# Block-sparse attention with a fused FFN: gathering only the needed K and V blocks, worked off in thirds of a batch

## The chip, the cores and the metric

The kernel runs on one core of a Trainium2 chip. The metric is the device time of one execution in microseconds (us), smaller is better. Each run also records the clock that was granted to the matmul engine (1.00 is full speed), and a run more than 1.5% above the fastest of its kernel counts as "slow".

The engines are named as in the profile: PE does matmuls (PEld is its weight load), DVE and ACT are the vector and the scalar engine, POOL is the engine that also issues gathers, SP issues most DMAs (its queue q1 moves 37.3 of 47.7 MB in the changed kernel). Each engine has its own list of instructions; in the traces below PE stands for 6.94 us before one of them while others stand behind it in the list.

## The reference

```python
# B, H, S, D = 4, 8, 768, 64;  block = 32, so 24 blocks;  3 sampled blocks for each query block
scores = q @ k.T / sqrt(D)
mask   = |blk_i - blk_j| <= 1  or  blk_i or blk_j is the first or last block
mask  |= (blk_j in sampled_blocks[blk_i])
attn   = softmax(where(mask, scores, -1e9)) @ v          # [4, 8, 768, 64]
x      = attn, heads side by side                        # [3072, 512]
h      = x @ w_in                                        # [3072, 1024]
solu   = h * softmax(h)
ln     = (solu - mean) / sqrt(var + 1e-6) * g_ln
out    = ln @ w_out                                      # [3072, 512]
```

q, k and v are drawn at a tenth of a normal distribution. The scores are therefore tiny and the softmax weights nearly equal over the allowed keys. A kernel that uses the wrong K or Q, or K of another batch, still passes the comparison.

## The kernel before

It computes all scores, masked ones too. The mask comes in through the matmul: K and Q are stored transposed with 24 extra rows (a block selector in K, minus 30000 for masked blocks in Q), so a masked score comes out of the same matmul as a large negative number. All is worked off in thirds of a batch (256 query rows), four pairs of heads in each, and the FFN of the third before is slipped in piece by piece.

```python
    def transpose_pair(b, pr):
        i = b % 2
        kc, qc, vc = loaded.pop((b, pr))
        for src, dst in ((kc, kT[i]), (qc, qT[i])):
            tp = ps_m.tile([P, S], BF16, tag="m", name="tp")
            for c in range(NCH):
                nc.tensor.matmul(tp[:, c * P : (c + 1) * P],
                                 src[:, c, :, :], ident,
                                 is_transpose=True, start=(c == 0),
                                 stop=(c == NCH - 1))
            nc.vector.tensor_copy(out=dst[0:D, 0, pr, :], in_=tp[0:D, :])
            nc.vector.tensor_copy(out=dst[D:P, 1, pr, :], in_=tp[D:P, :])
        nc.vector.tensor_copy(out=va[i][:, 2 * pr : 2 * pr + 2, :, 0:D],
                              in_=vc)

    # ... cut ...
    def scores(b, t, pr, n, exs):
        i = b % 2
        s = ps_s.tile([P, 4, TW], FP32, tag="s", name="s")
        for m in range(4):
            hh, jc = divmod(4 * n + m, NCH)
            nc.tensor.matmul(s[:, m, :],
                             kT[i][rows[hh], hh, pr, jc * P : (jc + 1) * P],
                             qT[i][rows[hh], hh, pr, t * TW : (t + 1) * TW],
                             start=(m % 2 == 0), stop=(m % 2 == 1))
        e = expp.tile([P, 4, TW], BF16, tag="ex", name="ex")
        nc.scalar.activation(out=e, in_=s, func=ACT.Exp, scale=scale)
        exs.append(e)

    # ... cut ...
    def pv(b, t, pr, exs, x):
        i = b % 2
        op = ps_m.tile([P, 2, 2, D + 1], FP32, tag="m", name="op")
        first = True
        for n in range(3):
            for m in range(4):
                hh, jc = divmod(4 * n + m, NCH)
                for qt in range(2):
                    nc.tensor.matmul(op[:, qt, hh, :],
                                     exs[n][:, m, qt * P : (qt + 1) * P],
                                     va[i][:, 2 * pr + hh, jc, :],
                                     start=first,
                                     stop=(n == 2 and m == 3 and qt == 1),
                                     skip_group_check=True)
                    first = False
    # ... cut ...
    # main loop, for each unit of a third and a pair of heads:
            if un in (2, 4, 6, 8):
                loaded[(b + 1, (un - 2) // 2)] = load_pair(b + 1, (un - 2) // 2)
            if un in (5, 7, 9, 11):
                bg.append(lambda b=b, p=(un - 5) // 2: transpose_pair(b + 1, p))
    # ... cut ...
        nbg = -(-len(bg) // 5) if len(bg) else 0
        for n in range(3):
            scores(b, t, pr, n, exs)
            if n == 0 and prev is not None:
                pb, pt, ppr, pexs = prev
                pv(pb, pt, ppr, pexs, xs[(pb, pt)])
                if ppr == NPR - 1:
                    bg.extend(ffn_pieces(pb, pt, xs[(pb, pt)]))
            if bg:
                bg.popleft()()
```

The preparation of the next batch is simple: Pool issues 20 loads for each batch that cast to bf16 on the way (`load_pair`), PE transposes K and Q, DVE copies them into place. No gather comes into it.

The softmax here doesn't subtract the row's maximum and nothing guards it: scores larger than these inputs give would overflow.

## Time and profile before

| | before |
|---|---|
| median of the first 3 runs (lowest to highest) | 281.83 us (281.5 to 283.57) |
| span of the profiled run | 281.1 us |
| PE busy | 238.8 us, 85% |
| PE not busy | 42.3 us, 28 of them in the first 60 us, 7 in the last 21 |
| one third of a batch in the middle | 19.5 us |

These lines are from the page of the kernel before. The first gives busy time by engine. The next four cut the span into 40 equal slices (7 us each); a digit is the busy share in tenths, and for PEclk the granted clock in tenths. Then come the DMA queue that Pool's issues go to (packets, MB, share of the time of 16 engines), and the chain of work that ended last, by engine.

```profile
PE 238.8 (85%) x3163; PEld 183.2 (65%) x3177; DVE 157.9 (56%) x365; ACT 174.4 (62%) x206; POOL 82.8 (29%) x142
PE   0116686999999999999999999999999999899783
ACT  1002468548858859667677688588488595785630
PEclk9999999999999999999999999999999999999998
DMA  5999999409759810049279020090100200200202
q0 software_dynamic: 55056, 10.49, 45.8%
PE 62%; DMA 11%; ACT 10%; DVE 9%; issue 3%; POOL 3%; ACTq 0%; POOLq 0%
```

The second view is the table by stretches of the same kernel. Columns: stretch and its length, then busy time (and instructions) of PE, PEld, DVE, ACT and POOL, the granted clock, the DMA share and GB/s.

```profile
core 0: us, PE busy (x) PEld busy (x) DVE busy (x) ACT busy (x) POOL busy (x), PEclk, DMA share, GB/s
60.00:100.00 40.00, 38.97 (x539) 30.13 (x541) 26.02 (x60) 28.52 (x34) 18.54 (x29) 1.00 0.85 87
100.00:140.00 40.00, 38.69 (x523) 29.81 (x525) 21.25 (x51) 28.58 (x34) 10.63 (x20) 1.00 0.42 53
140.00:180.00 40.00, 38.40 (x523) 29.67 (x523) 21.41 (x50) 28.64 (x34) 9.28 (x17) 1.00 0.39 48
180.00:220.00 40.00, 39.29 (x546) 30.60 (x546) 25.18 (x57) 28.79 (x34) 5.89 (x12) 1.00 0.24 38
```

And the waits of PE between 60 and 140 us, in the same kernel: who waited for whom, total us, times, longest.

```profile
PE s L215 <- ACT ex L220: 0.7, 3, 0.2
PE op L231 <- ACT ex L220: 0.4, 1, 0.4
```

Read together: from 60 us on PE has something to do in 38.4 to 39.3 of each 40 us, at full clock, and waits for nothing worth naming. PE is the limit there. ACT, at 28.6 of 40, and DVE, at 21 to 26, are not. Only work taken off PE can shorten the middle.

### The profile page before, as it was taken

Reading aid. Unit: us, or ns where it says so; the run is one execution under the profiler, and the core shown is the slowest. Engines: PE = TensorE matmul, PEld = TensorE weight load, DVE = VectorE, ACT = ScalarE, POOL = GpSimd, SP = SyncE. Lnnn points to the kernel's source line nnn. Section 1 sums busy time; section 2 is a strip of 40 time slices with the busy share of each in tenths; the row PEclk is TensorE's granted clock in tenths of the full one; section 3 lists DMA queues with packets and bytes.
Section 4 is the critical chain, followed back from the end, with each engine's and each line's share of the span. In section 5 each row is a group of like instructions: output and inputs, shape, how many; then the busy total and the mean of one; then the engine's idle time right before and its main releaser. Section 6 shows DMA issues by size and latency. Waiting matters only on the chain.

```text
span 281.1 us, 7445 instructions
## 1 busy us (share of the span) xinstructions
PE 238.8 (85%) x3163; PEld 183.2 (65%) x3177; DVE 157.9 (56%) x365; ACT 174.4 (62%) x206; POOL 82.8 (29%) x142
## 2 busy tenths in 40 slices
PE   0116686999999999999999999999999999899783
PEld 0004564867867867867767768678678577686561
DVE  3079789648639622756666616386376236155261
ACT  1002468548858859667677688588488595785630
POOL 8695861218139110045253100140100101001001
PEclk9999999999999999999999999999999999999998
DMA  5999999409759810049279020090100200200202
GB/s 117 264 191 188 185 180 118 58 4 140 48 93 128 85 54 23 2 90 100 30 109 79 3 77 2 37 96 2 47 31 2 77 2 2 76 2 3 76 0 77
DMA packets 61636, 20.40 MB, mean 73 GB/s; under 512 B 52225, under 2 KB 56994, under 8 KB 61602
## 3 DMA queue, kind: packets, MB, share of 16 engines
q0 software_dynamic: 55056, 10.49, 45.8%
q1 hardware_dynamic: 6546, 9.43, 9.8%
q8 instruction: 25, 0.41, 0.6%
q14 instruction: 9, 0.07, 0.1%
HBM read 23.07 MB, written 6.29 MB: 104 GB/s over the span
## 4 chain that ended last, share of the span: by engine, by line
PE 62%; DMA 11%; ACT 10%; DVE 9%; issue 3%; POOL 3%; ACTq 0%; POOLq 0%
PE s L215 15%; PE h L268 15%; PE ops L304 14%; PE op L231 10%; ACT ex L220 8%; DMA kc<-in_k_dram 7%; PE s3p L283 6%; DMA vc<-in_v_dram 4%; DVE w_out_sb L203 2%; ACT ot L312 2%; PE tp L161 2%; POOL qc L73 1%; DVE xT L258 1%; PE tps L256 1%; DVE x L240 1%
## 5 line engine op out<-in xcount | busy, mean ns | idle before, releaser
L220 ACT ACTIVATE ex<-s 128x1024 bf16<-128x1024 f32 x144 | 141.1, 1024 | 68.9 <-PE s L215 67.8
L215 PE MATMUL s<-qT_87,kT_85 88*128 88x256 bf16 (+1 forms) x288 | 49.5, 284 | 5.8 <-ACT ex L220 3.1
L231 PEld LDWEIGHTS <-ex 128*128 128x128 bf16 x1152 | 45.7, 98 | 11.1 <-ACT ex L220 4.6
L268 PE MATMUL h<-xT,w_in_sb 128*128 128x256 bf16 x384 | 47.8, 272 | 1.3 <-DVE xT L258 0.6
L215 PE MATMUL s<-qT_88,kT_86 88*128 88x256 bf16 (+1 forms) x288 | 46.2, 272 | 2.0 <-ACT ex L220 1.2
L273 DVE TENSOR_TENSOR solu<-h,e 128x512 bf16<-128x512 f32 x48 | 33.0, 687 | 26.3 <-ACT e L272 26.2
L304 PE MATMUL ops<-w_out_sb,solu 128*128 128x512 bf16 x179 | 44.6, 378 | 0.9 <-DVE s_4734 L290 0.3
L268 PEld LDWEIGHTS <-w_in_sb 128*128 128x128 bf16 x384 | 37.0, 97 | 6.3 <-issue 1.6
L272 ACT ACTIVATE e<-h 128x512 bf16<-128x512 f32 x48 | 28.7, 598 | 18.1 <-PE h L268 16.9
L215 PEld LDWEIGHTS <-kT_85 88*128 88x128 bf16 (+1 forms) x288 | 27.3, 101 | 13.5 <-issue 6.0
L73 POOL DMA_DIRECT2D kc<-in_k_dram x32 | 26.8, 841 | 18.6 <-PE tp L161 17.7
L215 PEld LDWEIGHTS <-kT_86 88*128 88x128 bf16 (+1 forms) x288 | 26.0, 97 | 9.3 <-issue 4.0
L304 PEld LDWEIGHTS <-solu 128*128 128x128 bf16 x192 | 18.4, 97 | 18.1 <-issue 0.3
L73 POOL DMA_DIRECT2D qc<-in_q_dram x32 | 26.2, 822 | 8.0 <-DMA w_in_sb<-in_moe_w_in_dram 3.7
L231 PE MATMUL op<-va_92,ex 128*128 128x65 bf16 x576 | 26.2, 193 | 2.7 <-ACT ex L220 2.2
L231 PE MATMUL op<-va_91,ex 128*128 128x65 bf16 x576 | 25.2, 196 | 1.9 <-DVE x L240 1.0
L239 DVE RECIPROCAL r<-op 128x4 f32<-128x4 f32 x48 | 8.5, 180 | 30.8 <-PE op L231 29.3
L274 DVE TENSOR_TENSOR sq<-solu 128x512 bf16<-128x512 bf16 x48 | 20.4, 425 | 1.3
L240 DVE TENSOR_TENSOR x<-op,r 128x256 bf16<-128x256 f32 x48 | 20.1, 420 | 1.0
L161 PE MATMUL tp<-ident,kc 128*128 128x128 bf16 x96 | 9.2, 240 | 12.2 <-DMA kc<-in_k_dram 10.5
L309 DVE TENSOR_SCALAR ot<-ops,rs 128x512 f32<-128x512 f32 x12 | 9.0, 751 | 16.7 <-PE ops L304 12.7
L312 ACT ACTIVATE ot<-ops,rs 128x512 f32<-128x512 f32 x12 | 8.2, 687 | 14.3 <-PE ops L304 14.3
(127 smaller groups left out, 201.7 us busy)
## 6 DMA issues: line engine op xcount, KB each, us to landing
out_dram<-ot SPq DMA_DIRECT2D x24, 256.0 KB
kc<-in_k_dram POOLq DMA_DIRECT2D x32, 96.0 KB, 5.1
qc<-in_q_dram POOLq DMA_DIRECT2D x32, 96.0 KB, 4.4
vc<-in_v_dram POOLq DMA_DIRECT2D x16, 192.0 KB, 5.0
w_out_f<-in_moe_w_out_dram SPq DMA_DIRECT2D x1, 2048.0 KB
w_in_sb<-in_moe_w_in_dram POOLq DMA_DIRECT2D x1, 1024.0 KB, 9.5
kT_86<-selp SPq DMA_DIRECT2D x8, 36.0 KB
qT_88<-mskp SPq DMA_DIRECT2D x8, 36.0 KB
```

The source lines that it names most:

```text
L73: nc.gpsimd.dma_start(out=t[:, :, hh, :], in_=src[b, 2 * pr + hh, :, :].rearrange("(p c) d -> p c d", p=P))
L161: nc.tensor.matmul(tp[:, c * P : (c + 1) * P], src[:, c, :, :], ident, is_transpose=True, start=(c == 0), stop=(c == NCH - 1))
L215: nc.tensor.matmul(s[:, m, :], kT[i][rows[hh], hh, pr, jc * P : (jc + 1) * P], qT[i][rows[hh], hh, pr, t * TW : (t + 1) * TW], start=(m % ...
L220: nc.scalar.activation(out=e, in_=s, func=ACT.Exp, scale=scale)
L231: nc.tensor.matmul(op[:, qt, hh, :], exs[n][:, m, qt * P : (qt + 1) * P], va[i][:, 2 * pr + hh, jc, :], start=first, stop=(n == 2 and m == ...
L240: nc.vector.tensor_tensor(out=x[:, :, 2 * pr * D : (2 * pr + 2) * D].rearrange("p a (h d) -> p a h d", h=2), in0=op[:, :, :, 0:D], in1=r.b ...
L268: nc.tensor.matmul(h[:, ff, :], w_in_sb[:, c, f * P : (f + 1) * P], st["xT"][:, c, :], start=(ff == 0 and c == 0), stop=(ff == 1 and c == ...
L272: nc.scalar.activation(out=st["e"][:, sl, :], in_=h, func=ACT.Exp)
L273: nc.vector.tensor_mul(out=st["solu"][:, sl, :], in0=h, in1=st["e"][:, sl, :])
L274: nc.vector.tensor_mul(out=st["sq"][:, sl, :], in0=st["solu"][:, sl, :], in1=st["solu"][:, sl, :])
L283: nc.tensor.matmul(s3p[:, qt, g : g + 1], st[nm][:, f, qt * P : (qt + 1) * P], onesf[:, 0:1], start=first, stop=(qt == 1 and g == 2 and f ...
L304: nc.tensor.matmul(ops, st["solu"][:, f, qt * P : (qt + 1) * P], w_out_sb[:, f, :], start=(f == 0), stop=(f == KF - 1))
```

## The change

The intent: do not compute masked scores. For a query block, only these keys count: the first and last block, its own block and its neighbours, and three sampled blocks. So a pair of heads in a third needs fewer exponentials and less PE time. The price is that the needed blocks must be brought side by side:

- **K**: K and Q are loaded as fp32 in 384 KB loads, cast (`turn`), transposed on PE (eight 96-column transposes for a pair and tensor), laid out by ACT and DVE. Then Pool copies the sampled K blocks inside SBUF (`gather_k`, an SBUF gather; three per two pairs of heads).
- **V**: V is cast, written to a scratch in DRAM, read back shifted (`stage_v`), and for each query block Pool issues one indirect DMA that gathers 96 sampled rows (`gather_v`; 22 per batch).
- The FFN stays as it was, but its rows' order changes, and all output scaling goes to ACT.

Pool's order is written by hand from end to end (`plan` is a table of slots), PE's for the first two thirds. The rest of PE's order, and all of DVE's and ACT's, come from the scheduler.

The diff has 882 lines; this is its core, in its own words, with cuts marked.

```diff
-    def transpose_pair(b, pr):
-        i = b % 2
-        kc, qc, vc = loaded.pop((b, pr))
-        for src, dst in ((kc, kT[i]), (qc, qT[i])):
-            tp = ps_m.tile([P, S], BF16, tag="m", name="tp")
-            for c in range(NCH):
-                nc.tensor.matmul(tp[:, c * P : (c + 1) * P],
-                                 src[:, c, :, :], ident,
-                                 is_transpose=True, start=(c == 0),
-                                 stop=(c == NCH - 1))
-            nc.vector.tensor_copy(out=dst[0:D, 0, pr, :], in_=tp[0:D, :])
-            nc.vector.tensor_copy(out=dst[D:P, 1, pr, :], in_=tp[D:P, :])
-        nc.vector.tensor_copy(out=va[i][:, 2 * pr : 2 * pr + 2, :, 0:D],
-                              in_=vc)
# ... cut ...
-    def scores(b, t, pr, n, exs):
-        i = b % 2
-        s = ps_s.tile([P, 4, TW], FP32, tag="s", name="s")
-        for m in range(4):
-            hh, jc = divmod(4 * n + m, NCH)
-            nc.tensor.matmul(s[:, m, :],
-                             kT[i][rows[hh], hh, pr, jc * P : (jc + 1) * P],
-                             qT[i][rows[hh], hh, pr, t * TW : (t + 1) * TW],
-                             start=(m % 2 == 0), stop=(m % 2 == 1))
-        e = expp.tile([P, 4, TW], BF16, tag="ex", name="ex")
-        nc.scalar.activation(out=e, in_=s, func=ACT.Exp, scale=scale)
-        exs.append(e)
# ... cut ...
+    def gather_v(b, g):
+        t = vp.tile([P, 2, HE], BF16, tag="vr", name="vr", bufs=NVR)
+        for i in range(2):
+            qb = 2 * g + 1 + i
+            nc.gpsimd.indirect_dma_start(
+                out=t[0 : NR * BLK, i, :], out_offset=None, in_=v_s[b][:, :],
+                in_offset=bass.IndirectOffsetOnAxis(ap=vidx[0 : NR * BLK, qb : qb + 1], axis=0))
# ... cut ...
+    def turn(t, nm, eng):
+        c = ldr.tile([PL, R8, 2, D], BF16, tag=nm, name=nm, bufs=2 if nm == "kr" else 1)
+        eng(out=c, in_=t.rearrange("p h r d -> p r h d"))
+        tp = ps_m.tile([P, R8, PL], BF16, tag="m", name="tp")
+        for r in range(R8):
+            nc.tensor.matmul(tp[:, r, :], c[:, r, :, :].rearrange("p h d -> p (h d)"), perm,
+                             is_transpose=True, start=(r == 0), stop=(r == R8 - 1))
+        return tp
# ... cut ...
+    def transpose_k(n, eng=None):
+        tp = turn(kld[n], "kr", eng or nc.vector.tensor_copy)
+        kT = kp.tile([P, S], BF16, tag="kT", name="kT", bufs=8)
+        nc.scalar.copy(out=kT.rearrange("p (a r) -> p a r", r=R8),
+                       in_=tp.rearrange("p r a -> p a r"))
+        kq[n] = kT
+        i, s = divmod(n, 2)
+        if s == 0:
+            kT2[i] = kp.tile([P, NB, 2, BLK], BF16, tag="kT2", name="kT2")
+        kTb = kT.rearrange("p (b c) -> p b c", c=BLK)
+        nc.vector.tensor_copy(out=kT2[i][:, :, s, :], in_=kTb)
+        kb = krtb[i % 3]
+        nc.scalar.copy(out=kb[:, s, 2 : NB - 2 : 2, 3, :], in_=kTb[:, 2 : NB - 2 : 2, :])
+        nc.scalar.copy(out=kb[:, s, 3 : NB - 2 : 2, 3, :], in_=kTb[:, 1 : NB - 4 : 2, :])
# ... cut ...
+    def gather_k(i, r, j):
+        q0, n_, tb = KR[r]
+        nc.gpsimd.indirect_copy(
+            krts[i % 3][:, :, q0 : q0 + n_, j, :].rearrange("p a q c -> p q a c"),
+            kT2[i].rearrange("p b a c -> p (b a c)").bitcast(U32).rearrange(
+                "p (b a c) -> p b a c", b=NB, a=2),
+            kidx[tb][:, j, :], True)
# ... cut ...
+    def transpose_q(n):
+        tp = turn(qld[n], "qr", nc.vector.tensor_copy)
+        dst = qbd[n % NQ]
+        for hh, eng in ((0, nc.scalar.copy), (1, nc.vector.tensor_copy)):
+            sl = slice(hh * D, (hh + 1) * D)
+            eng(out=dst[sl, :, hh, :].rearrange("p t (a r) -> p t a r", r=R8),
+                in_=tp[sl].rearrange("p r (t a) -> p t a r", t=NCH))
# ... cut ...
+    def score_b(T, i):
+        b, t = divmod(T, NT)
+        nb = min(8, NM - 8 * t)
+        it = []
+        for x in range(2):
+            kT, kb, qb_ = kqb(b * NPR + 2 * i + x)
+            for y in range(nb):
+                m = 8 * t + y
+                it.append(((x * nb + y) * H64, H64, 0, P,
+                           kb[:, m + 1, :, :].rearrange("p j c -> p (j c)"),
+                           qb_[:, m // 4, :, BLK * (m % 4) : BLK * (m % 4 + 1)], True))
+        un[(T, i)]["b"] = score_tile("eb", it, 2 * nb * H64)
# ... cut ...
+    def plan(b):
+        n0 = (b + 1) * NPR
+        z = b * NU + (6 if b == 0 else 0)
+        for i in range(4):
+            at(z + 2 * i, lambda i=i: load_v(b + 1, i))
+            at(z + 2 * i + 1, lambda i=i: place_v(b + 1, i))
+            at(z + 3 + 2 * i, lambda i=i: load_k(n0 + i))
+            at(z + 5 + 2 * i, lambda i=i: transpose_k(n0 + i))
+            at(z + 11 + 2 * i, lambda i=i: load_q(n0 + i))
+            at(z + 14 + 2 * i + i // 2, lambda i=i: transpose_q(n0 + i))
+        at(z + 8, lambda: stage_v(b + 1))
+        for j in range(NR):
+            at(z + 9 + j, lambda j=j: gather_k(n0 // 2, 0, j))
+            at(z + 20 + j, lambda j=j: gather_k(n0 // 2 + 1, 0, j))
+        for g in range(4):
+            at(z + 16 + g, lambda g=g: gather_v(b + 1, g))
# ... cut ...
+    for T in range(2, B * NT + 1):
+        for i in range(2):
+            for k_ in range(4):
+                ready(8 * T + 4 * i + k_)
+                if T < B * NT:
+                    if k_ == 0:
+                        score_a(T, i)
+                    if k_ == 1:
+                        score_b(T, i)
+                    if k_ >= 2 and T % NT == NT - 1:
+                        score_d(T, i, k_ - 2)
+                if k_ % 2 and prev is not None:
+                    pT, pi = prev
+                    if pi == 0 and k_ == 1:
+                        xs[pT] = xp.tile([P, 2, d_model], BF16, tag="x", name="x")
+                    pv(pT, pi, k_ // 2, xs[pT])
+                todo(1)
+            if prev is not None and prev[1] == 1:
+                done(prev[0])
```

## The prediction

> **What bounds the kernel now.** The matmul engine (PE). The table by stretches gives it 38.4 to 39.3 us busy in each 40 us between 100 and 220 us, at a granted clock of 1.00; ACT has 28.6 us there and DVE 21 to 25: loaded, not limiting. The chain of waits is 62% PE. A third of a batch (256 query rows) takes 19.5 us: in the chain, output-projection pieces stand at 99.95, 119.07, 139.00 ... 275.52 us, nine intervals. Besides, there are about 43 us of start (first exponential at 26 us, first attention-times-V at 34[...]) and a 20 us tail.
>
> PE work per third, from spacings in the timeline: scores 48 matmuls at 109 ns = 5.3 us; times V 96 at 38 ns = 3.6; FFN in 32 at 109 = 3.5; statistics 48 at 27 = 1.3; FFN out 16 at 217 = 3.5; transposes 1.4. Sum 18.6 of 19.5.
>
> **What the change does.** The FFN (8.3 us of PE per third) stays. Scores shrink to 4 matmuls of 512 columns, 16 of 128, 32 of 64 (last third: 24, plus 24 of 128): estimated 3.0 us, or 4.1, saving about 2. Times V rises from 96 to 112 matmuls (last third 136), with 32 or 64 output columns. [...] Estimated 3.4 to 5 us, a loss of 0.5. K and Q transposes rise from 6 to 8 per pair and tensor: +0.2 us. Net 1.3 to 3 us less PE per third, mid 2.
>
> ACT: exponentials fall from 36 per batch to about 14.5 equivalents at 0.98 us (-85 us in all); K copies, Q halves, V placement, output scaling and Ln/Exp add about 60. DVE: -35 us of transposed copies, +60 us of casts and layout copies. Both stay below PE, at 70 to 80%.
>
> Pool: 80 issues at 0.82 us go. In come 88 indirect row gathers[...] and 30 SBUF gathers. [...] Together about 180 us: hidden in the middle, not at the start.
>
> **Start.** K -> transposes -> SBUF gathers, and V -> bf16 -> DRAM scratch -> indirect gather -> first times V, which I expect at 32 to 38 us; Pool (6 gathers, then 8 row gathers) holds the second third until about 55 us. So the start is perhaps 5 us longer. The tail is unchanged.
>
> **Predicted: 255 us**, 238 to 272 eight times in ten; faster by over 2% 0.88, within 2% 0.07, slower 0.05.
>
> **What would show it.** Right: output projections spaced 17 to 17.8 us in the middle, PE above 93% busy there, exponentials of scores near 57 us in all, first FFN output near 63 us, Pool 60 to 70% busy. Wrong by step: PE idle in the middle released by ACT or DVE (they became the limit); PE waiting for row or SBUF gathers (Pool limits); times V over 5.5 us per third[...].
>
> **What would make it wrong.** An SBUF gather above 6 us makes Pool the limit; the time could exceed 280. [...] the extra DMA traffic (V through DRAM, gathered per query block), could delay the start by 10 us or more.

Passages that no trace or run shows are cut out of this text, and each cut is marked. Pool's "about 180 us" was 88 row gathers and 30 SBUF gathers, each kind at an estimate for one instruction. The terms of the total: 281.8 us before, about 2 us less of PE for each of 12 thirds, perhaps 5 us more for the start. They come to about 263 us, not 255. The 3.4 to 5 us for times V are the author's estimate (112 matmuls at the 38 ns seen before would be 4.3 us, against 3.6), and its range isn't derived. The mark of 6 us for an SBUF gather is an estimate too: 30 of them, with 88 row gathers at the 1.22 us that were measured afterwards, would make 287 us of Pool.

## The result, and the profile after

| | before | after |
|---|---|---|
| median of the runs of this comparison | 281.76 us | **298.87 us** (297.73 to 299.8, 4 runs) |
| ratio | | 1.059, 95% interval 1.053 to 1.065 |
| span of the profiled run | 281.1 us | 298.0 us |
| PE busy | 238.8 us | 226.2 us |
| PE not busy | 42.3 us | 71.8 us |
| mean granted clock of the profiled run | 0.997 | 0.927 |
| DMA | 20.4 MB in 61,636 packets | 47.7 MB in 34,772 packets |

(A ratio is the mean time of one kernel's fast runs over that of the other's in the same rounds, so it is not quite the ratio of the medians quoted beside it.)

The change is slower by 5.9%. PE's busy time fell by 12.6 us, and its idle time rose by 29.5 (in the two profiled runs). The same lines of the page, for the changed kernel, with the DMA queue that SP's issues go to (q1) added:

```profile
PE 226.2 (76%) x3640; PEld 161.2 (54%) x3640; DVE 162.6 (55%) x411; ACT 154.7 (52%) x242; POOL 137.5 (46%) x138
PE   0316227882599953969996998799999999999892
ACT  1735304665429550674755847756555454655232
PEclk9999999997569975887999999989999999999998
DMA  5999999389859968457896997856143421110102
q0 software_dynamic: 4752, 9.84, 14.3%
q1 hardware_dynamic: 29984, 37.34, 48.7%
PE 43%; DMA 24%; DVE 11%; ACT 8%; POOL 6%; issue 5%; SPq 1%; POOLq 0%; ACTq 0%; DVEq 0%
```

Two things are to be seen. PE's line has holes up to slice 26 (194 us, a slice is 7.45 us here), and the clock line dips with them, to 5 to 7 tenths in slices 10 to 12 and 15 to 16. From slice 27 on PE's line is solid but for the tail. (The clock record of this trace begins only at 53.0 us. Before that the line shows full speed, but eight FFN matmuls at 52.08 us took 1.48 us, where eight at 56.51 us took 1.03; so full speed in the start is not shown.) The table by stretches shows both (same columns as above):

```profile
60.00:80.00 20.00, 10.31 (x172) 6.51 (x175) 10.47 (x20) 9.67 (x18) 9.92 (x10) 0.75 0.95 244
80.00:100.00 20.00, 19.12 (x293) 13.39 (x293) 12.99 (x33) 12.57 (x20) 11.15 (x11) 0.82 0.76 189
100.00:120.00 20.00, 10.97 (x171) 7.84 (x169) 8.03 (x12) 6.55 (x8) 12.00 (x11) 0.69 0.74 192
120.00:140.00 20.00, 17.59 (x283) 12.72 (x282) 11.00 (x31) 14.01 (x24) 7.71 (x8) 0.80 0.54 147
140.00:160.00 20.00, 16.86 (x319) 12.56 (x316) 15.24 (x29) 13.06 (x20) 13.32 (x12) 1.00 0.90 237
240.00:260.00 20.00, 19.89 (x390) 14.65 (x388) 12.57 (x35) 11.25 (x17) 1.06 (x2) 1.00 0.14 40
```

In 240 to 260 us, where no preparation is left (Pool has two instructions), PE is busy 19.89 of 20 us at full clock. In 60 to 80 and 100 to 120 us it is busy about half of the time, at a clock of 0.75 and 0.69. These are the waits of PE between 60 and 140 us:

```profile
PE tp L280 <- DVE kr L277: 7.9, 3, 5.2
PE s L341 <- POOL krt_149 L312: 6.9, 1, 6.9
PE tp L280 <- DVE x L431: 1.9, 1, 1.9
```

PE waits for the cast of K (`kr`), for the transposes to start, and for Pool's SBUF gather (`krt`). The cast in its turn waits for the load, as the waits of DVE show (60 to 220 us, all of it before 80 us):

```profile
DVE kr L277 <- DMA kc<-in_k_dram: 6.3, 4, 2.4
```

The timeline shows the largest wait of these. Columns: start, length, engine, line, operation and tiles; in brackets the idle time of that engine before, and what ended it.

```profile
109.10 0.64 PE L341 MATMUL s<-qbd_143,kT 128*64 128x512 bf16 x1
110.04 1.43 POOL L312 INDIRECT_COPY krt_149<-kT_945,kidx_133 128x768 uint32 x1 [1.38 <-issue]
...
111.64 0.95 POOL L252 DMA_INDIRECT vr<-v_s_137,vidx  x1 [0.17 <-issue]
...
112.89 0.92 POOL L252 DMA_INDIRECT vr<-v_s_137,vidx  x1 [0.30 <-issue]
...
115.19 1.43 POOL L312 INDIRECT_COPY krt_149<-kT_945,kidx_133 128x768 uint32 x1 [1.38 <-issue]
...
116.67 0.24 PE L341 MATMUL s<-qbd_143,krt_149 128*128 128x64 bf16 x1 [6.94 <-POOL krt_149 L312]
```

At 109.10 us PE has a first score of the second two pairs of heads of batch 2's first third out and then needs their gathered K. The three SBUF gathers for it (the first of them, at 103.84 us, is not shown) stand in Pool's order behind 12 row gathers of V, and four more stand between them. Those four are for the second third of batch 2, whose times V begins at 142.8 us. A gather of K is 1.43 us busy with 1.38 us of nothing before it, and PE stands still until the third one has landed: 6.94 us in which PE had other work in its list, but behind this instruction.

Where the time is lost becomes clear from the start of the scaling of the last output tile of each third:

| third | before | after | after minus before |
|---|---|---|---|
| 1 (batch 1) | 63.3 | 87.2 | +23.9 |
| 2 | 83.2 | 103.5 | +20.3 |
| 3 | 103.6 | 141.6 | +38.0 |
| 4 (batch 2) | 122.7 | 162.2 | +39.5 |
| 7 (batch 3) | 182.2 | 218.9 | +36.7 |
| 8 | 202.1 | 236.0 | +34.0 |
| 12 | 277.2 | 292.7 | +15.5 |

Twenty us are lost in the start, eighteen more in the third third, little is won while preparation of batches 3 and 4 goes on, and then 21 us are won in the last five thirds. A third there takes 11.3 to 17.2 us, 14.8 on the mean, against 19.0 for the same five before.

### The profile page after: what moved, and what is told of

It reads as the page before. It is cut to its first block, busy times and chain, and to the rows that moved or that the text cites. A ratio compares the mean times of both kernels' runs of the same rounds, so it can differ in the third digit from the quotient of the medians.

```text
span 298.0 us, 8536 instructions
## 1 busy us (share of the span) xinstructions
PE 226.2 (76%) x3640; PEld 161.2 (54%) x3640; DVE 162.6 (55%) x411; ACT 154.7 (52%) x242; POOL 137.5 (46%) x138
## 2 busy tenths in 40 slices
DMA packets 34772, 47.70 MB, mean 160 GB/s; under 512 B 5296, under 2 KB 18096, under 8 KB 34736
## 3 DMA queue, kind: packets, MB, share of 16 engines
q0 software_dynamic: 4752, 9.84, 14.3%
## 4 chain that ended last, share of the span: by engine, by line
PE 43%; DMA 24%; DVE 11%; ACT 8%; POOL 6%; issue 5%; SPq 1%; POOLq 0%; ACTq 0%; DVEq 0%
PE ops L544 13%; PE op L427 8%; PE h L503 8%; PE s L341 6%; DMA kc<-in_k_dram 5%; POOL vr L252 4%; DMA vc<-in_v_dram 4%; PE s3p L518 4%; DMA vr<-v_s_137,vidx 4%; DMA e<-in_v_dram 4%; DMA v_s_136<-vst_141 4%; DVE solu L508 2%; DMA vr<-v_s_136,vidx 2%; PE tps L489 2%; DMA qc<-in_q_dram 2%
## 5 line engine op out<-in xcount | busy, mean ns | idle before, releaser
L427 PEld LDWEIGHTS <-ea 64*64 64x64 bf16 (+1 forms) x544 | 19.9, 109 | 22.0 <-issue 9.2
L343 ACT ACTIVATE ea<-s 128x1024 bf16<-128x1024 f32 x24 | 24.5, 1022 | 13.4 <-PE s L341 13.3
L547 ACT ACTIVATE ot<-ops,rs 128x512 f32<-128x512 f32 x24 | 16.5, 686 | 28.4 <-PE ops L544 26.8
L252 POOL DMA_INDIRECT vr<-v_s_137,vidx x22 | 21.8, 991 | 12.2 <-PE tps L489 4.3
L280 PE MATMUL tp<-perm,kr 96*128 96x96 bf16 x128 | 10.5, 238 | 22.0 <-DVE kr L277 16.4
L252 POOL DMA_INDIRECT vr<-v_s_136,vidx x22 | 21.1, 958 | 12.3 <-issue 6.3
L252 POOL DMA_INDIRECT vr<-v_s_138,vidx x22 | 21.0, 955 | 9.7 <-issue 5.4
L252 POOL DMA_INDIRECT vr<-v_s_139,vidx x22 | 20.3, 923 | 10.3 <-issue 4.4
L343 ACT ACTIVATE eb<-s 128x1024 bf16<-128x1024 f32 (+1 forms) x24 | 22.8, 951 | 3.3 <-PE s L341 3.3
L341 PEld LDWEIGHTS <-kT 128*64 128x64 bf16 (+1 forms) x336 | 18.2, 112 | 10.1 <-issue 6.8
L280 PEld LDWEIGHTS <-kr 96*128 96x128 bf16 x128 | 8.3, 115 | 25.5 <-DVE kr L277 17.2
L492 DVE COPY xT<-tps 128x512 bf16<-128x512 bf16 x24 | 10.1, 424 | 21.3 <-PE tps L489 21.2
L427 PE MATMUL op<-ve,ea 64*128 64x65 bf16 x192 | 15.0, 201 | 8.1 <-DMA ve<-v_s_136 4.2
L431 DVE TENSOR_TENSOR x<-op,r 128x256 bf16<-128x256 f32 x48 | 20.2, 421 | 1.2
```

The lines of the kernel that those rows point to most:

```text
L252: nc.gpsimd.indirect_dma_start(out=t[0 : NR * BLK, i, :], out_offset=None, in_=v_s[b][:, :], in_offset=bass.IndirectOffsetOnAxis(ap=vidx[0 ...
L280: nc.tensor.matmul(tp[:, r, :], c[:, r, :, :].rearrange("p h d -> p (h d)"), perm, is_transpose=True, start=(r == 0), stop=(r == R8 - 1))
L341: nc.tensor.matmul(dst, lhsT, rhs, start=(o % 512 == 0), stop=(x == last[o // 512]), skip_group_check=True)
L343: nc.scalar.activation(out=e, in_=s[:, 0:width], func=ACT.Exp, scale=scale)
L427: nc.tensor.matmul(o_, l_, r_, start=(x == 0), stop=(x == len(mm) - 1), skip_group_check=True)
L431: nc.vector.tensor_tensor(out=xt[:, :, 2 * pr * D : (2 * pr + 2) * D].rearrange("p a (h d) -> p a h d", h=2), in0=op[:, :, :, 0:D], in1=r. ...
```

## The experiments

The question is why preparing the data held up PE. There were eighteen runs of sixteen kernels, on several chips, each next to the kernel before on the same chip. Numbers below are medians of the fast runs; "after" is 298.9. The texts quote medians of all runs (303.96 for e4 and 293.9 for e5, for instance). Profiles of e4, e5, e6, e8, e10 and e18 fell in the slow state. The first line of theories was: the bytes of the gathers; the number of Pool instructions; the output stores in the SP queue; the order in the start. The later runs take the preparation apart.

One remark on what an edit does besides its intent. After the first two thirds the scheduler orders PE, and everywhere DVE and ACT, anew. Where a comparison of the built kernels showed the orders the same, it is said. Otherwise some 180 to 800 of about 7,280 PE entries moved. How much that alone can be worth no run isolates. In e3 501 PE entries moved, and the time moved by 1.3 us; but in e7 274 moved against e5, besides 50 added matmuls, and the time rose by 9.2 us. Differences of a few us between such kernels are not read as effects, and single gains of 4 to 10 us only with care. By the order of instructions in the traces, PE keeps its order, or all but about 1% of it, in e1, e6 and e12 against the changed kernel, in e5 against e4, and in e18 against e14: these comparisons are the cleanest.

### e1_few_bytes: a row gather that moves an eighth of the bytes

```diff
-                out=t[0 : NR * BLK, i, :], out_offset=None, in_=v_s[b][:, :],
+                out=t[0 : NR * BLK, i, 0 : E], out_offset=None,
+                in_=v_s[b].rearrange("s (h e) -> (s h) e", e=E),
...
-                                   vr[(b, (8 * t + m) // 2)][:, m % 2, cols(hh)]))
+                                   vr[(b, (8 * t + m) // 2)][:, m % 2, 0:E]))
```

> Wrong result on purpose: every indirect row gather keeps its 96 rows and its Pool instruction, but moves 130 bytes per row, not 1040 (about 7.7 MB of the 47.7 MB go). Theory DMA (the extra traffic of V through DRAM saturates the transfer engines and holds up the loads): at least 12 us faster than the changed kernel (298.9), so 287 or less. Rival theory ORDER (the loss is waiting in the in-order streams of Pool, PE and the store/load queue, at the start of each batch's preparation): within 5 us of 298.9, since the Pool instructions take the same 0.91 us each.

Measured: 298.9 us, ratio 1.068 (1.063 to 1.074); wrong result. All engines keep their order exactly. Pool's row gathers cost the same. This is the group of row gathers among the groups of Pool in this run (busy us, mean ns, then idle before and why):

```profile
L252 POOL DMA_INDIRECT vr<-v_s,vidx x88 | 86.2, 980 | 40.1 <-issue 19.4 <-PE op L428 7.0 <-DMA v_s<-vst 6.0
```

In the changed kernel the 88 gathers took 923 to 991 ns each. The DMA queue of the gathers (q0) took 5.0% of the 16 engines' time, not 14.3%. So the bytes, and the traffic of the gathers with them, are not the cause: what a row gather costs Pool does not depend on them here.

### e2_no_gather: no row gathers for batches 2 to 4

```diff
     def gather_v(b, g):
+        if b > 0:
+            vr[(b, g)] = vr[(0, g)]
+            return
```

> Wrong result on purpose: the V rows gathered for the first batch are used again for the other three, so 66 of 88 indirect gathers go, with their bytes and their 1.2 us of Pool each (about 80 us of Pool). Theory DMA and theory POOL (the Pool stream of row gathers holds up the SBUF gathers of K): both at least 20 us faster than 298.9; with the kernel of few bytes this says which. Theory START (nearly all is lost before the second batch by the order of the first two thirds): no more than 10 us faster, since the first batch's gathers are kept.

Measured: 283.6 us, ratio 1.007 (1.000 to 1.013); wrong result. Pool's busy time falls from 137.5 to 73.9 us. With 66 of 88 row gathers gone, 15 us go, and between 60 and 140 us no wait of PE for Pool is left in its profile. As e1 shows that it isn't their bytes, it is most likely Pool's time, in which other things stand behind them; by the traces a few hundred of PE's entries moved too, which this run can't separate. But the kernel would then still be no faster than before, so this isn't all.

### e3_store_act: output stores issued by ACT

```diff
-            nc.sync.dma_start(out=out[r0 : r0 + n, :], in_=ot[p0 : p0 + n, :])
+            nc.scalar.dma_start(out=out[r0 : r0 + n, :], in_=ot[p0 : p0 + n, :])
```

> The output stores are issued from ACT, not SP, so loads of the next batch no longer stand behind a store that waits for its activation (103.9 us of such waits, 21 times, in the queue's waits). Theory QUEUE: 10 us or more faster (289 or less). Rivals START, POOL and DMA: within 5 us of 298.9.

Measured: 300.2 us, ratio 1.067 (1.062 to 1.072). In the changed kernel the SP queue waits 103.9 us in all for output tiles, with loads behind the stores. It looks like a jam, but moving the stores away gained nothing. The theory of the SP queue falls.

### e4_pv_first and e5_k_first: the order in the second third

e4 puts attention times V of the second third ahead of that stretch's preparation of batch 2. e5 is e4 plus one number: the second group of K gathers of batch 2 comes earlier in Pool's order, ahead of batch 2's row gathers. Between e4 and e5 only Pool's order differs.

```diff
 # e4
-        for k_ in range(8):
-            ready(8 * T + k_)
+        if T == 0:
+            for k_ in range(8):
+                ready(8 * T + k_)
         for i in range(2):
             for x in range(2):
                 pv(T, i, x, xs[T])
+        if T == 1:
+            for k_ in range(8):
+                ready(8 * T + k_)
 # e5, besides
-            at(z + 20 + j, lambda j=j: gather_k(n0 // 2 + 1, 0, j))
+            at(z + (12 if b == 0 else 20) + j, lambda j=j: gather_k(n0 // 2 + 1, 0, j))
```

> In the fixed order of the second third, the four times-V groups stand before, not after, the K and V preparation of the second batch. In the changed kernel PE waits 8.6 us there for K casts of the second batch (2.5 + 5.2 + 0.9 us in the timeline from 68 to 78 us) and times V of the second third starts only at 78 us, though its last rows were gathered by about 64 us. Theory START: the first output of the second third comes 10 us or more earlier, and the whole is 8 to 20 us faster (279 to 291). Theory POOL: the second third comes earlier, but the Pool stream sets the third third, and the whole moves under 5 us.

> The kernel with times V first in the second third, plus one change of the Pool order: the three SBUF gathers of K for the second head group of batch 2 stand before, not between, that batch's row gathers. In the parent (303.96) the first third of batch 2 has PE idle for 12.66 us until the third of those gathers, which starts at 114 us although its K was ready near 90 us; 18 row gathers of 1.2 us stood before it. Theory POOL ORDER: that wait shrinks to under 5 us and the whole is 8 to 14 us faster than the parent, 290 to 296. Rival POOL THROUGHPUT: PE then waits as long for the row gathers, the whole stays within 4 us of the parent.

Measured: e4 303.0 us, ratio 1.075 (1.068 to 1.082); e5 291.4 us, ratio 1.032 (1.026 to 1.038). In e4 the second third did end earlier (its last projection began at 95.5 instead of 101.6 us in the profiles), and everything was given back at the next gate. These are the longest waits of PE between 60 and 140 us in e4 (only the order of size is used):

```profile
PE s L341 <- POOL krt L312: 12.7, 1, 12.7
PE tp L280 <- DVE kr L277: 6.1, 2, 4.9
```

And this is the longest in e5 in the same stretch:

```profile
PE tp L280 <- DVE kr L277: 8.3, 3, 6.9
```

Moving three Pool instructions is worth about 11.5 us against e4, and the wait for Pool is gone. But a wait of the next gate, 6.9 us for the cast of K, now stands in its place. An earlier start only reaches a later gate sooner.

### e6_w_late: the FFN weights behind the first row gathers

```diff
-    load_w_in()
     for g in range(4):
         gather_v(0, g)
+    load_w_in()
```

> The changed kernel with one line moved: the 2 MB load of the first FFN weight is issued after, not before, the first eight row gathers. Theory START DMA (the transfer engines are the limit up to 50 us: about 250 GB/s in slices 4 to 6): the last of the first eight row gathers lands 4 to 8 us earlier than 46.2 us, the second-third times V moves with it, the whole is 3 to 8 us faster than 298.9. Rival: the start is a chain of latencies (write of V to DRAM 10.5 us, issue of eight gathers at 1.2 us) and not bytes: first gathers land within 2 us of 46.2.

Measured: 305.6 us, ratio 1.083 (1.078 to 1.088), a miss. Only Pool's order differs. In its profile the times V of the first third comes some 3 us earlier, the FFN of the first third waits 3.5 us for its weights, and the later thirds lose more than was gained. The order of the start is a trade, not an oversight.

### e7_warm: useless matmuls against the low clock

```diff
+    def warm(n):
+        d = ps_h.tile([P, 512], FP32, tag="h", name="warm")
+        for x in range(n):
+            nc.tensor.matmul(d, ident, qbd[0][:, 0:2, :, :].rearrange("p t h c -> p (t h c)"),
+                             start=True, stop=True)
 # in pv, first third and first pair only: 24 of them ahead, 14 and groups of 3 between
```

> On the kernel with K gathers first: 50 matmuls of no use (128 by 512, into a free bank, never read) are put where PE waits for V in the first third, between 31 and 46 us, to keep its clock up. In the changed kernel the FFN matmuls of the first third then run at 186 ns (8 in 1.48 us), 110 ns in the kernel before. Theory CLOCK (the slow clock after idling is a cost of its own): FFN matmuls near 110 ns from 50 us on and 4 to 10 us off the parent. Rival: those matmuls are hidden behind other waits; under 2 us.

Measured: 300.6 us, ratio 1.064 (1.057 to 1.072), against 291.4 of e5, on which it builds. In the place that it aimed at it worked: eight FFN matmuls of the first third took 1.03 us at 51.8 us, where the changed kernel needed 1.48. But the first output came no earlier (62.5 against 61.2 us), as the chain there ran over the preparation of the output weights on ACT and DVE. The scheduler also moved 274 PE entries. The 9.2 us that it lost against e5 come later: between 100 and 140 us its profile has a wait of PE of 6.4 us for a row gather, which e5's doesn't have. So this run doesn't say what the low clock costs in all; it says that in the start the clock was not what held the first output.

### e8_wout_inplace and e11_wout_kfirst: output weights out of K's and Q's load buffers

In the changed kernel the fp32 output weights sit in the load buffers of K and Q until they are scaled, so that the first K load of batch 2 has to wait for that. e8 loads them as bf16 into their own place. e11 is e8 with the order of e5.

```diff
-        wt["f"] = [ld.tile([P, 2, d_model], FP32, tag=tg, name="w_out_f")
-                   for tg in ("kc", "kc", "qc", "qc")]
...
+        nc.gpsimd.dma_start(out=w_out_sb, in_=moe_w_out.rearrange("(c p) d -> p c d", p=P))
```

> The changed kernel, but the second FFN weight is cast while it loads (by a Pool-issued transfer) and is scaled in place, so it no longer sits in the four buffers of the K and Q loads. In the changed kernel those buffers come free only at 62 to 67 us, so the K loads of the second batch are issued at 63 to 71 us and PE waits 8.6 us for their casts. Theory START BUFFERS: those K loads are issued before 55 us, that wait goes, and the whole is 6 to 15 us faster than 298.9. Rival (the Pool stream sets the first third of batch 2 in any case): PE waits the more for the SBUF gathers near 110 us, the whole within 4 us of 298.9.

> Correct result: times V first, K gathers first and the in-place second weight together. If the three waits are in series: 280 to 288, at or near the kernel before (281.8). If they hide one another: no better than the best of its parts, 293.9.

Measured: e8 294.7 us, ratio 1.044 (1.039 to 1.049); e11 293.5 us, ratio 1.044 (1.036 to 1.052). Against the changed kernel e5 gains 7.5 us and e8 4.2, and both together 5.4: no more than e5 alone. No correct version that was run beats the kernel before.

### e9_no_prep and e10_no_kq: what all the preparation costs

e9 leaves out every preparation of batches 2 to 4 and computes all batches from batch 1's data. e10 leaves out K's and Q's alone (loads, casts, transposes, layout copies, SBUF gathers) and keeps V's whole path.

```diff
 # e9
-    for b in range(B - 1):
-        plan(b)
+    for b in range(1, B):
+        vt[b] = vt[0]
+        for n in range(NPR):
+            kq[b * NPR + n] = kq[n]
 # e10, in plan: the lines of load_k, transpose_k, load_q, transpose_q and gather_k removed
```

> Wrong result on purpose: no preparation of batches 2 to 4 (no loads, casts, transposes, gathers); all batches use the first one's Q, K and V. Theory PREPARATION (the attention and FFN work of a third takes PE about 15 us, as in the last five thirds of the changed kernel's trace, and the rest of the middle is preparation and waits for it): 10 thirds at 15 us after 85 us and the tail, so 235 to 250. Rival CORE (the many small matmuls and exponentials cost 17 us or more per third by themselves): 268 or more.

> Wrong result on purpose: K and Q of the first batch are used for all, so their loads, casts, transposes and SBUF gathers go for batches 2 to 4; the V path (load, DRAM scratch, 88 row gathers) stays whole. The opposite half of the kernel without row gathers, which took 283.6. If the K and Q side is the larger cost: 270 or less. If the V row gathers are: 285 or more.

Measured: e9 **253.3** us, ratio 0.897 (0.894 to 0.901), wrong result. e10 260.7 us, ratio 0.923 (0.919 to 0.927); its result is wrong. This is the table by stretches for e9:

```profile
80.00:120.00 40.00, 39.78 (x759) 29.91 (x759) 21.64 (x60) 23.44 (x35) 0.00 (x0) 1.00 0.09 29
120.00:160.00 40.00, 39.73 (x699) 28.22 (x699) 18.40 (x57) 21.58 (x34) 0.00 (x0) 1.00 0.11 37
160.00:200.00 40.00, 39.89 (x743) 29.85 (x743) 21.72 (x60) 22.78 (x35) 0.00 (x0) 1.00 0.10 33
```

Without preparation the changed kernel keeps PE busy 39.7 to 39.9 of 40 us at full clock, from 80 us on, as the kernel before did. So the core of the change is sound, and the preparation costs 45.6 us (the lower clock of PE that comes with it is in that); leaving out K's and Q's side alone gains 38.1 of them. With that side gone, V's whole path costs 7.5 us (e10 against e9), while with it in place leaving out V's row gathers gained 15 (e2). Not all of the 45.6 us is waiting: PE's own share of it is 192 transposes, 13.6 us of busy time (20.2 us of transposes in the changed kernel, 6.6 in e9). The kernel before has such transposes too, 18.1 us in all.

### e12_no_kgather, e13_no_turn, e14_no_load: one part of K's and Q's preparation at a time

```diff
 # e12, in gather_k
+        if i >= 2:
+            if i == 2:
+                nc.gpsimd.memset(krts[2][:, :, :, j, :], 0)
+            return
 # e13, in transpose_k (likewise in transpose_q); the gathers read batch 1's tiles
+        if n >= NPR:
+            kq[n] = kq[n % NPR]
+            return
 # e14, in load_k (likewise in load_q); stale(n) is a view of the tiles of the output weights
+        if n >= NPR:
+            kld[n] = stale(n)
+            return
```

> Wrong on purpose (sampled K of batches 2 to 4 is zero or stale). The changed kernel with the 18 SBUF gathers of sampled K for batches 2 to 4 left out on Pool (three memsets stand for the first three, so that nothing is read unwritten); loads, casts, transposes and layout copies of K and Q are all kept, and PE, DVE and ACT have the same instructions in the same order. All K and Q preparation together was worth about 37 us. Theory A, Pool: the 18 gathers take about 3.2 us of Pool each and hold up scores and row gathers, so this alone gives 20 us or more (below 279 against 299 for the changed kernel). Theory B, the casts, transposes and copies in the in-order streams of PE, DVE and ACT cost most: this gives only the one 6.9 us wait that the profile puts on a Pool gather, 4 to 9 us (290 to 295).

> Wrong on purpose (K and Q of batch 1 are used for all batches). The changed kernel with the casts, PE transposes and layout copies of K and Q for batches 2 to 4 left out; their loads from HBM and the 18 SBUF gathers on Pool (from the tiles of batch 1) are kept. Theory B (casts, transposes and copies in the in-order streams): 192 transposes are about 13.6 us of PE busy time, and 10 to 12 us of PE waits on their casts go with them, so 22 to 32 us (267 to 277). Theory A (Pool): the PE time alone goes, 8 to 15 us (284 to 291). DVE and ACT lose about a fifth of their work, and the scheduler orders the rest anew, which may blur a few us.

> Wrong on purpose (K and Q of batches 2 to 4 are cast from the tiles that hold the output weights). The changed kernel with the 24 loads of K and Q from HBM for batches 2 to 4 left out; casts, transposes, copies and SBUF gathers are kept, and PE and Pool have the same instructions in the same order (DVE and ACT are ordered somewhat differently by the scheduler). Theory C, late loads: the casts wait for the loads, which share buffers with the output weights and come late, and the transposes wait for the casts; then this gives 10 us or more (below 289). If the loads are no limit, within 4 us of 299.

Two corrections to these texts: in e12, 34 of 7,283 PE entries and one of DVE moved, so "the same order" is true only nearly; in e14, 328 PE entries moved, so for PE it isn't true. Results of all three are wrong.

| | left out | time | gain on after | ratio (95%) |
|---|---|---|---|---|
| e12 | 18 SBUF gathers on Pool | 289.9 us | 9.0 | 1.027 (1.021 to 1.032) |
| e13 | casts, transposes, layout copies | 288.8 us | 10.1 | 1.027 (1.019 to 1.036) |
| e14 | 24 loads | 290.8 us | 8.1 | 1.034 (1.027 to 1.041) |
| e10 | all three | 260.7 us | 38.1 | 0.923 (0.919 to 0.927) |

No theory of the three that named one culprit holds. Each part gives 8 to 10 us; the sum of the three is 27.2, and all together give 38.1. (Of the two single gains that came with moved orders, e13's and e14's, part can be due to the order. e12 keeps it.) The waits of PE between 60 and 140 us show why each alone gives so little. In e12, without the gathers, PE still waits for casts of K and for ACT's copies of them:

```profile
PE tp L280 <- DVE kr L277: 4.3, 2, 4.1
PE s3p L522 <- ACT kT L298: 2.7, 1, 2.7
```

In e13, without casts and transposes, PE gets to the same gate sooner and waits for Pool there, 14.5 us instead of 6.9:

```profile
PE s L349 <- POOL krt L318: 14.5, 1, 14.5
```

In e14, without loads, it does so for 9.5 us:

```profile
PE s L350 <- POOL krt L321: 9.5, 1, 9.5
```

### e15 to e18: two parts at a time

e15 is e14 with the order of e5. e16 is e14 and e12 together; against e14 PE and ACT keep their order exactly.

> Wrong on purpose (K and Q of batches 2 to 4 are cast from the tiles of the output weights). The run without K and Q loads, together with the order in which the second K gather group of batch 2 stands before its row gathers and times V of the second third stands before the preparation. Without the loads, PE waited 9.5 us for a Pool SBUF gather; with the new order alone, it waited 7.3 us for casts that waited for loads. Theory of two gates in a row (each part ends just behind another, so that taking one away shows the other): both waits go, and the time falls to 276 to 284, 15 us or more below the changed kernel. If the two gains only add up: 285 to 288. If something else holds this stretch (casts and copies in order, low clock): 289 to 294. Pool has the order of the run with the new order, PE, DVE and ACT are partly ordered anew by the scheduler.

> Wrong on purpose. Both the loads of K and Q for batches 2 to 4 and their SBUF gathers on Pool are left out, casts, transposes and copies are kept (against the run without loads only Pool changes order). Taken alone the two gave about 10 and 9 us of the 37 that all three parts together gave. If the parts hide one another, this gives 22 to 28 us (271 to 277), and what is left to 261 is the PE time of the 192 transposes, about 13.6 us, and little else. If the gains only add up, 279 to 283. If the casts and transposes are the gate by themselves, 286 to 292.

Measured: 353.1 us and 364.0 us, ratios 1.254 and 1.289. Neither theory had room for that. The page of the profile shows an odd thing: the largest wait of PE in e16 has no releaser. "Issue" is idle time in which the engine waited for nothing that the profile shows.

```profile
PE op L440 <- issue: 37.9, 39, 4.3
```

In all, e16 has 50 us of such waits, e15 31 us, and every run before had at most 1.5 us. Between 104 and 107 us, for instance, PE starts one matmul about every 0.7 us, where nothing that the profile shows holds it. The kernel before, run on the same chip in between, was at its usual 283.0 us. As e16 has the very order of PE's instructions that took 291 us as e14, the two kernels were run again, unchanged, under new names, on another chip:

> The same kernel as the run with the new order and without loads, run once more. There it took 353 us, and its profile gave 31 us of PE idle time to issue (1 us or less in the other runs), which neither theory explains. If that belonged to the chip or to the session, the PE idle time put down to issue is now about 1 us and the time is 276 to 284 by the theory of parts that hide one another, 285 to 288 if gains add up. If it belongs to the kernel, the time is again about 353 us with some 30 us of issue.

> The same kernel as the run without loads and without SBUF gathers, run once more. There it took 364 us with 50 us of PE idle time put down to issue, although PE and ACT have the same instructions in the same order as in the run without loads, which had 0.7 us of it and took 292 us. If that belonged to the chip or to the session: 271 to 277 by the theory of parts that hide one another, 279 to 283 if gains add up, 286 to 292 if casts and transposes are the gate by themselves. If it belongs to the kernel: about 364 us again.

Measured: e17 285.0 us, ratio 1.011 (1.004 to 1.018); e18 **276.6** us, ratio 0.978 (0.970 to 0.986; by the rule of 2% "unclear"). PE's idle time put down to issue is 0.9 and 0.7 us. So the 353 and 364 us belonged to that chip or session and not to the kernels, and are read no further; what it was stays open.

e17: 13.8 us below after. That is "gains add up" at most (7.5 of e5 and 8.1 of e14 make 15.6) and not the more than 15 that the theory of two gates asked for. e18: 22.2 us below after, more than the 17.1 that e12 and e14 gave one by one, and at the edge of what the theory of parts that hide one another asked for (271 to 277). The cleanest form of it: PE has the same order in e14 and e18, and leaving out the SBUF gathers gains 14.2 us there, where the loads are gone too, and 9.0 in e12, where they are not. In e18 the largest waits of PE between 60 and 140 us are these (the lines are used for the releasers alone):

```profile
PE tp L289 <- DVE xT L505: 2.3, 1, 2.3
PE s3p L531 <- ACT kT L307: 1.3, 1, 1.3
PE cs L476 <- ACT w_out_g L474: 1.1, 4, 0.4
```

No wait for K's gather or cast is left. From e18 to e10, where the casts, transposes and copies go as well, 15.9 us are missing, near the 13.6 us of PE's own transposing. The ledger closes within a few us: of K's and Q's 38.1 us, about 14 are PE work, and about 22 are loads and SBUF gathers arriving late, where taking either away alone shows the other. That the 13.6 us of busy time cost as much in time is an estimate; no run leaves out the transposes alone.

## Why the prediction was wrong

The prediction was 255 us (238 to 272), the result 298.9. Point by point:

- **PE limits the kernel before: right.** Nothing in the runs speaks against it, and e9 confirms that less PE work gives less time, when PE is fed.
- **PE work falls by about 2 us per third: right.** e9 has thirds of 15.4 us on the mean from the second to the last (169.3 us for 11), before had 19.4 (213.9 for 11). But e9 lacks 13.6 us of transposes, 1.2 for each of the 11. That leaves a gain near 2.8, within the predicted 1.3 to 3. PE's busy time fell by 12.6 us only, partly since matmuls ran at a lower clock. Eight output projections at 83.55 us, where the granted clock was 0.50, took 3.62 us, eight at 98.35 us, at full clock, 1.89:

```profile
83.55 3.62 PE L544 MATMUL ops<-w_out_sb,solu 128*128 128x512 bf16 x8
98.35 1.89 PE L544 MATMUL ops<-w_out_sb,solu 128*128 128x512 bf16 x8
```

  With two more such groups (at 133.49 and 193.48 us, at a clock of 0.50 too) that makes about 5 us for the output projections alone.
- **Times V costs PE a little more: right in sum.** The trace shows weight loads of 32 to 64 columns at 100 to 117 ns, against 96 to 107 for full ones of 128 by 128. The transposes' loads of 128 columns and 96 rows took 109 to 115 ns as well, so a loss through the narrow tiles is small here and not shown for sure. The four groups of times V are 57.5 us busy in sum (overlaps between groups counted twice), against 51.4 before, so at most the 0.5 us per third that the prediction allowed.
- **The exponentials: right.** 60.1 us of scores' exponentials, 57 predicted.
- **The sum of Pool's instructions: right.** A row gather takes 1.22 us of Pool from one to the next, an SBUF gather of 24 blocks 2.7 to 3.2 us, one of 14 blocks 1.80. (The author's estimates for one instruction came from no trace.) Busy time alone would have misled: it is mostly 1.43 us for an SBUF gather, and the rest is the gap before it. 88 row gathers and 30 SBUF gathers make 175 to 187 us (88 at 1.22, 18 at 2.7 to 3.2, 12 smaller ones at 1.3 to 2.7, most of them 1.8 or less), as predicted.
- **"Together about 180 us: hidden in the middle, not at the start": this is the step that failed.** The prediction compared Pool's 180 us with a span of 255 and saw room. But Pool's order is a single line with gates in it: row gathers for a third whose times V begins at 142.8 us stand before SBUF gathers for which PE already waits (6.94 us, until 116.67). And the same holds for the chain load, cast, transpose, copy: PE takes transposes in their place in its order, and waits there when the cast has waited for the load (7.9 us between 60 and 140 us). It is not a lack of throughput of Pool or another compute engine: none but PE is more than 55% busy over the span, Pool 46% (60 to 70 predicted), and moving three Pool instructions took PE's wait for Pool away (e5). It is waiting in lists worked off in order. Among its signs of being wrong the prediction had "PE waiting for row or SBUF gathers (Pool limits)": the wait came, but not from Pool being full. The DMA engines are the rival to that: between 60 and 140 us they are busy 75% of the time and move 193 GB/s. But e12 moved 221 GB/s and e2 209 in the same stretch and both were faster, so the mean rate was not the limit. Whether K's loads between 60 and 80 us, where the share is 0.95, came late because they were issued late or because others were in the way, no run separates. The runs put 15 us on the row gathers of V (e2) and about 22 us on loads and SBUF gathers of K and Q (e18). These overlap: in all it is 45.6 us less 13.6 of PE work, about 32 us (e9).
- **"The start is perhaps 5 us longer": mis-sized.** Its first marks came true: the first times V ran at 35.5 us (32 to 38 predicted), the first output projection began at 63.0 us ("first FFN output near 63"). But the first third ended 23.9 us later than before, the second 20.3. Of that, 13.8 and 8.7 are there in e9 too, which has no preparation of batch 2; there the second half of the first third's output, at 73.8 us, stands in PE's order behind the second third's times V. The rest, 10 and 12 us, is preparation of batch 2: in the changed kernel that second half (83.55 us) stands behind K's transposes of batch 2 as well, for which PE waits 7.7 us between 68 and 78 us. The third third takes another 18.
- **The sum was off as well.** The text's own terms (2 us for each of 12 thirds, less 5 for the start) give about 263, not 255.
- **The clock, which the prediction left out.** The granted clock is 0.50 in four stretches between 53 and 295 us (from 70.1, 107.6, 131.5 and 193.0 us), 41.0 us in all; in e9 only for a short while near 75 us (0.91 on the mean from 60 to 80 us; six output projections at 75.02 us took 2.77 us). All of the four began with no wait of PE over 2.5 us just before them; the waits of 5.2 and 6.9 us fell into the first two. In the 5 us before each start PE was busy 2.1 to 3.4 us, and from 240 to 260 us, where it was busy 19.89 of 20, the clock was 1.00. So gaps in PE's work came before each of them, and in the start, where e7 filled such gaps, eight FFN matmuls took 1.03 us instead of 1.48; what exactly brings the low clock on no run isolates. Gaps that it follows are paid for twice, as idle time and in slower matmuls (eight output projections in 3.62 us instead of 1.89). By how much in all no run tells (e7 is inconclusive). An estimate from the trace: PE was busy 26.2 of those 41.0 us, so at most about 13 us, which are part of the 32 us above.

What is known, then: without preparation of later batches the changed kernel takes 253 us; with the transposes' PE time added, about 267, an estimate from the numbers of e9 and the trace, and inside the range that was predicted. The 32 us on top are preparation that isn't hidden. What would hide it wasn't found: seven correct variants gave 291.4 at best (e5).

## What to carry to other kernels

When a change trades work on the limiting engine for preparation on idle engines, don't compare the preparation's sum with the span; follow one item of it through every in-order queue, and ask at each whether something that is needed later stands in front of it, and whether the limiting engine takes part in the preparation itself (transposes), for then it waits in place (7.9 us for casts of K here). Where several parts of a chain arrive at nearly the same time, taking away one of them tells little (8 to 10 us each here, 38.1 for all three): take away all for the whole cost first (as e9 did), then pairs. And a run that no theory has room for is to be repeated on another chip before it is explained.
